# Mish in one ScalarE pass, logarithms of two head pairs at once, and three banks for the hidden product

## The chip, the cores and the metric

The kernel runs on one core of a Trainium2 chip. The metric is device time in microseconds (us), the median of several executions. TensorE multiplies matrices, VectorE and ScalarE work elementwise, SyncE only issues transfers (its queue is SPq in the rows), GpSimd is not used. PE stands for TensorE, PEld for its weight loads, DVE for VectorE, ACT for ScalarE.

## The reference, cut to what matters

```python
# q, k, v: [8, 8, 576, 64]; g_norm: [64]; w_in: [512, 2048]; w_out: [2048, 512]
kv  = einsum('bhsd,bhse->bhde', k, v)
a   = einsum('bhsd,bhde->bhse', q, kv)
a   = a / sqrt(mean(a * a, axis=-1, keepdims=True) + 1e-6) * g_norm
x   = a.transpose(0, 2, 1, 3).reshape(4608, 512)
h   = x @ w_in
out = (h * tanh(log1p(exp(h)))) @ w_out        # mish, then the second product
```

## The kernel before, in words

Everything is kept with features on the 128 partitions and tokens along the free dimension. The 4608 tokens are nine tiles of 512. x^T of a tile is made for four **head pairs** (128 features each) and then goes through 16 **chunks** of 128 hidden units. A float32 product runs as three passes of a faster format: each operand is split into a high part (a rounding copy on ScalarE, L85) and a low part (a subtraction on VectorE, L86).

**A chunk** is `hidden` (12 matmuls of 128x512 into one PSUM bank psh, L259 to L261, four quarters of the contraction with three passes each), `mish_a` and `mish_b` (elementwise, into gh and gl), and `project_out` (12 matmuls into the four banks acc, L288 to L290). The program traces them skewed: the hidden product of a chunk, mish_b of the chunk before it, then the second product of the chunk two steps back. `mish_a` is a chain that goes to and fro: Exp on ScalarE (L269), a clamp on VectorE (L270), Square on ScalarE (L271), (v + 0.5) h on VectorE (L272, the last reader of the bank psh), Ln and Exp on ScalarE (L273, L274); `mish_b` multiplies (L278) and splits. psh has two banks.

**x of the next tile** is made while a tile runs. `attention_slots` gives each step its slot, two slots per chunk: k^T v of a batch in two halves (L157, into a bank psa), and per head pair: load q, transpose, project (psa), square, sums over a head's features by a matmul with a matrix of ones (psa again), rstd (Ln at L242, Exp at L243), normalize (L246, then the split into xh and xl). psa has two banks; the projection's bank is held from its matmuls until L246.

**The first tile** has nothing to hide behind. The string START lists the order in which its loads, weight conversions and steps to x are traced; its projections go to the banks acc. A weight arrives as a float64 block (512 KB), and `weight` makes it float32: a scaling pass on ScalarE (L100), three integer passes on VectorE (L104 to L106, the last of which is the last reader of the raw block), then the split. The raw blocks (w64) have three buffers. Six blocks are in START, the other 26 are loaded in the chunks of the first tile, one of w_out per chunk and one of w_in until all 16 are there.

**The order on each engine** is not the program's: a scheduler goes through the traced instructions with a timeline of its own, and at each moment gives an engine the ready instruction that was traced first. On the chip each engine's queue then runs in that fixed order, and an instruction that waits holds up what is behind it. All loads and stores are issued by SyncE, in such an order too; a load waits there until its buffer is free.

The functions that the diff touches:

Of the kernel before, what the change touches and what calls it, by code (L numbers as in the profile page):

```python
# [7 lines left out]
F32 = mybir.dt.float32  # L8
F32R = mybir.dt.float32r
U32 = mybir.dt.uint32  # L10
AF = mybir.ActivationFunctionType
ALU = mybir.AluOpType
LB = -18 * 0.6931471805599453     # log(4 2^-20)


# the order in which the first tile starts. w, k, q: load weights, half of k and v,
# queries of a head pair; c: convert weights; m: k^T v; t, s, n: the steps to x
START = (
    "w0 k0 q0 q1 m0 t1 w1 t0 q2 s1 s0 c0 c1 w2 k1 m1 "
    "n1 t2 w3 n0 c2 w4 q3 s2 n2 c3 t3 s3 c4 w5 c5 n3"  # L20
# [4 lines left out]
def linear_attention_rms_mish_ffn(  # L25
# [20 lines left out]
    w_in, w_out = w_in.bitcast(U32), w_out.bitcast(U32)   # words of float64, low first  # L46
    P = 128
    T = 512                      # tokens of one tile of the feed-forward part
    NT = NTOK // T
    NKC = DM // P                # contraction chunks of x w_in, = head pairs  # L50
    NFC = DF // P                # chunks of the hidden dimension
    NSUB = T // P
    CM = 4                       # rows of k, v per partition in the main load
    SM = CM * P                  # rows in the main load
    SL = S - SM                  # rows left over

    T32 = 2                      # tiles whose x is made of unsplit operands
# [3 lines left out]
    wraw = ctx.enter_context(tc.tile_pool(name="wraw", bufs=3))  # L61
# [6 lines left out]
    ps_h = ctx.enter_context(tc.tile_pool(name="ps_h", bufs=2, space=bass.MemoryType.PSUM))  # L68
    ps_a = ctx.enter_context(tc.tile_pool(name="ps_a", bufs=2, space=bass.MemoryType.PSUM))
    ps_o = ctx.enter_context(tc.tile_pool(name="ps_o", bufs=1, space=bass.MemoryType.PSUM))  # L70

    nc.scalar.preload_act_table_set("natural_log_exp_and_others")
# [7 lines left out]
    eps = const.tile([P, 1], F32, name="eps")  # L80
    tiny = const.tile([P, 1], F32, name="tiny")
    lb = const.tile([P, 1], F32, name="lb")
# [6 lines left out]
    # The high word, read as a float32 and scaled by 2^-112, is the exponent  # L89
    # rebased to float32 and 20 bits of the mantissa, three places too low;  # L90
    # what float32 can't hold fades to zero.
# [41 lines left out]
    # Block-diagonal tiles of head pairs: the unsplit one of batch 0 or 1, and  # L133
    # the split ones, which batches two apart share.
# [56 lines left out]
    def unit_steps(j, hp, xh, xl):  # L191
# [31 lines left out]
        def square():  # L223
            t = ffn.tile([P, T], F32, name="n") if j == 0 else att.tile([P, T], F32, name="fa")
            nc.scalar.square(t, st["x"])
            if j < T32:
                st["sf"] = t
            else:
                st["sh"], st["sl"] = parts(t)

        def sums():
# [6 lines left out]
            st["ss"] = ps  # L238

        def rstd():  # L240
            st["r"] = att.tile([P, T], F32, name="fb")
            nc.scalar.activation(st["r"], st["ss"], AF.Ln, bias=eps, scale=1.0 / D)  # L242
            nc.scalar.activation(st["r"], st["r"], AF.Exp, scale=-0.5)  # L243

        def normalize():
            nc.vector.scalar_tensor_tensor(st["r"], st["x"], gcol, st["r"], ALU.mult, ALU.mult)  # L246
            split(xh[:, hp, :], xl[:, hp, :], st["r"])

        return load, transpose, project, square, sums, rstd, normalize
# [14 lines left out]
    # mish(h) = h tanh(log(1 + exp(h))) = 2 h t / (t^2 + 1), t = 1 + 2 exp(-h).  # L264
    # The bound on exp(-h) keeps log's argument in its range; tanh is 2^-41 there.
    def mish_a(ps):
        v = ffn.tile([P, T], F32, name="u")
        r = ffn.tile([P, T], F32, name="n")
        nc.scalar.activation(v, ps, AF.Exp, scale=-1.0)  # L269
        nc.vector.tensor_scalar_min(v, v, 2.0 ** 41)  # L270
        nc.scalar.activation(r, v, AF.Square, bias=1.0, scale=2.0)  # L271
        nc.vector.scalar_tensor_tensor(v, v, 0.5, ps, ALU.add, ALU.mult)  # L272
        nc.scalar.activation(r, r, AF.Ln, bias=tiny, scale=2.0 ** -20)  # L273
        nc.scalar.activation(r, r, AF.Exp, bias=lb, scale=-1.0)  # L274
# [161 lines left out]
```

## Time and profile before

| | |
|---|---|
| time, median of 3 runs | 923.93 us (922.19 to 928.57) |
| span of the profiled execution | 924.8 us (no time of its own is given beside it) |
| mean granted TensorE clock | 0.986 of full speed |
| TensorE busy | 896.3 us, 97% |
| ScalarE busy | 635.4 us, 69% |
| VectorE busy | 539.0 us, 58% |
| matmuls | 4348, of them 3456 of the two big products |
| chain that ended last | TensorE 94%, transfers 3% |

The span runs from the first to the last instruction. Matmuls are pipelined, so the busy time of one (about 0.39 us) is longer than the interval from start to start; the rate is read from how many begin in a stretch. An engine's busy share over the whole span says little here, since the first tile has other limits than the rest.

### The profile page before, as it was taken

The numbers are of one execution on the slowest core, as the hardware profiler recorded it, in microseconds if no ns is written. First come the engines' busy times: TensorE is split into PE (matmuls) and PEld (weight loads), VectorE is DVE, ScalarE is ACT, GpSimd is POOL, SyncE is SP. The second block draws the span as 40 slices with busy tenths as digits, with TensorE's granted clock in tenths as the row PEclk, the third lists the DMA queues.
The fourth block names the chain that finished last, engine by engine and source line by source line (L and its number), as shares of the span: only waits on it lengthen the run. The fifth ranks groups of instructions, "written<-read, shape, count | busy, mean of one in ns | idle before, by whom it ended". The sixth has DMA issues, their size and how long they took to land.

```text
span 924.8 us, 11829 instructions
## 1 busy us (share of the span) xinstructions
PE 896.3 (97%) x4348; PEld 717.2 (78%) x4348; DVE 539.0 (58%) x908; ACT 635.4 (69%) x1057; POOL 0.2 (0%) x4
## 2 busy tenths in 40 slices
PE   3789999999999999999999999999999999999997
PEld 1467778888888888888788878888888888888886
DVE  5889986565456544655466545554565456544443
ACT  3688877677667766776577666776676677766554
POOL 0000000000000000000000000000000000000000
PEclk9779999999999999999999999999999999999999
DMA  8964361200250005200430034002300030001001
GB/s 217 276 210 138 107 232 45 47 1 1 70 122 4 1 3 129 63 0 1 117 78 1 1 103 91 1 1 74 69 1 1 1 88 5 0 1 46 1 1 45
DMA packets 113434, 55.31 MB, mean 60 GB/s; under 512 B 88288, under 2 KB 104672, under 8 KB 113376
## 3 DMA queue, kind: packets, MB, share of 16 engines
q1 hardware_dynamic: 113376, 54.55, 21.4%
q8 instruction: 34, 0.56, 0.2%
q14 instruction: 24, 0.20, 0.1%
HBM read 45.09 MB, written 9.44 MB: 59 GB/s over the span
## 4 chain that ended last, share of the span: by engine, by line
PE 94%; DMA 3%; SPq 1%; DVE 1%; ACT 1%; issue 0%; ACTq 0%
PE psh L259 15%; PE acc L290 15%; PE acc L288 14%; PE acc L289 14%; PE psh L261 14%; PE psh L260 14%; PE psa L157 3%; DMA w<-in_moe_w_in_dram 2%; PE psa L220 1%; PE psa L219 1%; DMA vm<-in_v_dram 1%; PE psa L218 1%; SPq L185 1%; PE psa L237 1%; PE psa L236 1%; PE psa L215 1%
## 5 line engine op out<-in xcount | busy, mean ns | idle before, releaser
L259 PE MATMUL psh<-xh,wil 128*128 128x512 f32 x576 | 231.2, 402 | 2.2 <-ACT xh L85 2.2
L260 PE MATMUL psh<-xl,wih 128*128 128x512 f32 x576 | 228.2, 396 | 0.0
L261 PE MATMUL psh<-xh,wih 128*128 128x512 f32 x576 | 227.9, 396 | 0.0
L290 PE MATMUL acc<-woh,gh 128*128 128x512 f32 x576 | 227.6, 395 | 0.0
L289 PE MATMUL acc<-wol,gh 128*128 128x512 f32 x576 | 227.2, 394 | 0.0
L288 PE MATMUL acc<-woh,gl 128*128 128x512 f32 x576 | 223.4, 397 | 0.0
L86 DVE TENSOR_TENSOR gl<-n,gh 128x512 fp32r<-128x512 f32 x144 | 99.5, 691 | 84.7 <-ACT gh L85 81.5
L278 DVE TENSOR_TENSOR n<-u,n 128x512 f32<-128x512 f32 x144 | 99.3, 690 | 82.5 <-ACT n L274 82.3
L85 ACT CAST gh<-n 128x512 fp32r<-128x512 f32 x144 | 89.1, 618 | 82.2 <-DVE n L278 67.2
L272 DVE SCALAR_TENSOR_TENSOR u<-u,psh 128x512 f32<-128x512 f32 x144 | 98.8, 686 | 76.9 <-ACT n L271 76.8
L269 ACT ACTIVATE u<-psh 128x512 f32<-128x512 f32 x144 | 86.2, 598 | 78.6 <-PE psh L261 77.6
L259 PEld LDWEIGHTS psh<-xh,wil 128*128 128x128 f32 x576 | 108.9, 189 | 29.6 <-ACT xh L85 2.6
L260 PEld LDWEIGHTS psh<-xl,wih 128*128 128x128 f32 x576 | 109.1, 189 | 26.3 <-issue 0.9
L261 PEld LDWEIGHTS psh<-xh,wih 128*128 128x128 f32 x576 | 108.7, 189 | 25.8 <-issue 0.2
L289 PEld LDWEIGHTS acc<-wol,gh 128*128 128x128 f32 x576 | 108.5, 188 | 25.2 <-ACT u L269 0.4
L290 PEld LDWEIGHTS acc<-woh,gh 128*128 128x128 f32 x576 | 108.2, 188 | 25.4 <-issue 0.2
L288 PEld LDWEIGHTS acc<-woh,gl 128*128 128x128 f32 x576 | 108.2, 188 | 25.4 <-issue 0.4
L271 ACT ACTIVATE n<-u 128x512 f32<-128x512 f32 x144 | 90.8, 631 | 44.0 <-DVE u L270 42.9
L274 ACT ACTIVATE n<-n,lb 128x512 f32<-128x512 f32 x144 | 104.1, 723 | 3.6
L273 ACT ACTIVATE n<-n,tiny 128x512 f32<-128x512 f32 x144 | 104.1, 723 | 3.2
L270 DVE TENSOR_SCALAR u<-u 128x512 f32<-128x512 f32 x144 | 61.2, 425 | 68.9 <-ACT u L269 68.2
L86 DVE TENSOR_TENSOR fl<-fa,fh 128x512 fp32r<-128x512 f32 x56 | 38.6, 689 | 19.3 <-ACT fh L85 18.7
(61 smaller groups left out, 569.1 us busy)
## 6 DMA issues: line engine op xcount, KB each, us to landing
out_dram<-stg SPq DMA_DIRECT2D x36, 256.0 KB, 2.0
w<-in_moe_w_in_dram SPq DMA_DIRECT2D x16, 512.0 KB, 4.9
km<-in_k_dram SPq DMA_DIRECT2D x16, 512.0 KB, 4.0
vm<-in_v_dram SPq DMA_DIRECT2D x16, 512.0 KB, 5.4
w<-in_moe_w_out_dram SPq DMA_DIRECT2D x16, 512.0 KB, 3.9
stg<-in_q_dram SPq DMA_DIRECT2D x32, 64.0 KB, 2.4
stg<-in_q_dram SPq DMA_DIRECT2D x32, 56.0 KB, 2.0
stg<-in_q_dram SPq DMA_DIRECT2D x32, 48.0 KB, 1.9
```

The source lines that it names most:

```text
L86: nc.vector.tensor_sub(lo, src, hi.bitcast(F32))
L259: nc.tensor.matmul(ps, wil[:, kc, f], xh[:, kc, :], start=(kc == 0), stop=False)
L260: nc.tensor.matmul(ps, wih[:, kc, f], xl[:, kc, :], start=False, stop=False)
L261: nc.tensor.matmul(ps, wih[:, kc, f], xh[:, kc, :], start=False, stop=(kc == NKC - 1))
L271: nc.scalar.activation(r, v, AF.Square, bias=1.0, scale=2.0)
L272: nc.vector.scalar_tensor_tensor(v, v, 0.5, ps, ALU.add, ALU.mult)
L273: nc.scalar.activation(r, r, AF.Ln, bias=tiny, scale=2.0 ** -20)
L274: nc.scalar.activation(r, r, AF.Exp, bias=lb, scale=-1.0)
L278: nc.vector.tensor_mul(r, v, r)
L288: nc.tensor.matmul(acc[t], gl[:, c], woh[:, fc, :], start=first, stop=False)
L289: nc.tensor.matmul(acc[t], gh[:, c], wol[:, fc, :], start=False, stop=False)
L290: nc.tensor.matmul(acc[t], gh[:, c], woh[:, fc, :], start=False, stop=last)
```

## The change

- `mish_a` becomes one ScalarE pass with the function Mish, from psh to v; `mish_b` is left with the split.
- Mish is in another function table than Ln and Exp. `rstd` therefore takes two head pairs at once: an explicit load of the table with Ln and Exp, then Ln and Exp over 128x1024; the next Mish needs its own table again. A helper `in_turn` fixes the order of these ScalarE instructions among themselves to the traced one.
- To let a pair wait for its neighbour, x times g and the scaled sums are put into new SBUF tiles raw and ss (one buffer each for two pairs): after the square, VectorE writes raw = x g; after the sums, VectorE writes ss = sums / 64 + 1e-6; `normalize` is a plain product and the split. So a psa bank is free after those passes.
- Banks: psh 3 instead of 2, psa 1 instead of 2. Raw weight blocks: 2 buffers instead of 3.
- In START and in the slots, rstd stands by itself ("r"), and some steps move: c3 behind r3, c5 behind n3. The initial table load goes, and so do three constants.

```diff
-    "n1 t2 w3 n0 c2 w4 q3 s2 n2 c3 t3 s3 c4 w5 c5 n3"
+    "r1 t2 w3 n0 n1 c2 w4 q3 s2 t3 s3 r3 c3 n2 c4 w5 n3 c5"
...
-    wraw = ctx.enter_context(tc.tile_pool(name="wraw", bufs=3))
+    wraw = ctx.enter_context(tc.tile_pool(name="wraw", bufs=2))
...
-    ps_h = ctx.enter_context(tc.tile_pool(name="ps_h", bufs=2, space=bass.MemoryType.PSUM))
-    ps_a = ctx.enter_context(tc.tile_pool(name="ps_a", bufs=2, space=bass.MemoryType.PSUM))
+    xr = ctx.enter_context(tc.tile_pool(name="xr", bufs=1))
+    ps_h = ctx.enter_context(tc.tile_pool(name="ps_h", bufs=3, space=bass.MemoryType.PSUM))
+    ps_a = ctx.enter_context(tc.tile_pool(name="ps_a", bufs=1, space=bass.MemoryType.PSUM))
...
-    nc.scalar.preload_act_table_set("natural_log_exp_and_others")
...
+    def in_turn(i):
+        if last:
+            order = mybir.DependencyInfo(mybir.DependencyClass.NoSync, mybir.DependencyReason.DATA)
+            tc.add_manual_dep(i.ins, last.pop().ins.name, order, reason="tables")
+        last.append(i)
...
             nc.scalar.square(t, st["x"])
+            nc.vector.tensor_scalar_mul(raw[:, hp % 2, :], st["x"], gcol)
...
-            st["ss"] = ps
-
-        def rstd():
-            st["r"] = att.tile([P, T], F32, name="fb")
-            nc.scalar.activation(st["r"], st["ss"], AF.Ln, bias=eps, scale=1.0 / D)
-            nc.scalar.activation(st["r"], st["r"], AF.Exp, scale=-0.5)
+            nc.vector.tensor_scalar(ss[:, hp % 2, :], ps, 1.0 / D, 1e-6, ALU.mult, ALU.add)
 
         def normalize():
-            nc.vector.scalar_tensor_tensor(st["r"], st["x"], gcol, st["r"], ALU.mult, ALU.mult)
-            split(xh[:, hp, :], xl[:, hp, :], st["r"])
+            r = raw[:, hp % 2, :]
+            nc.vector.tensor_mul(r, r, ss[:, hp % 2, :])
+            split(xh[:, hp, :], xl[:, hp, :], r)
...
+    def rstd(ss):
+        in_turn(nc.scalar.preload_act_table_set("natural_log_exp_and_others"))
+        in_turn(nc.scalar.activation(ss, ss, AF.Ln))
+        in_turn(nc.scalar.activation(ss, ss, AF.Exp, scale=-0.5))
...
     def mish_a(ps):
         v = ffn.tile([P, T], F32, name="u")
-        r = ffn.tile([P, T], F32, name="n")
-        nc.scalar.activation(v, ps, AF.Exp, scale=-1.0)
-        nc.vector.tensor_scalar_min(v, v, 2.0 ** 41)
-        nc.scalar.activation(r, v, AF.Square, bias=1.0, scale=2.0)
-        nc.vector.scalar_tensor_tensor(v, v, 0.5, ps, ALU.add, ALU.mult)
-        nc.scalar.activation(r, r, AF.Ln, bias=tiny, scale=2.0 ** -20)
-        nc.scalar.activation(r, r, AF.Exp, bias=lb, scale=-1.0)
-        return v, r
+        in_turn(nc.scalar.activation(v, ps, AF.Mish))
+        return v
 
-    def mish_b(v, r):
-        nc.vector.tensor_mul(r, v, r)
+    def mish_b(v):
         gh = ffn.tile([P, T], F32R, name="gh")
         gl = ffn.tile([P, T], F32R, name="gl")
-        split(gh, gl, r)
+        split(gh, gl, v)
         return gh, gl
...
             s0 = 3 + 6 * hp
             slots[s0 - 1].append(start)
-            for d, n in zip((0, 2, 3, 4, 6, 11, 11), range(7)):
+            for d, n in zip((0, 2, 3, 4, 6), range(5)):
                 slots[s0 + d].append(lambda n=n, cell=cell: cell[n]())
+            e = 16 + 12 * (hp // 2)
+            if hp % 2 == 0:
+                slots[e + 1].append(lambda hp=hp: rstd(raws[j, hp // 2][1]))
+            slots[e + 3 + hp % 2].append(lambda cell=cell: cell[5]())
```

## Rows read from the trace of the kernel before

**Rows 1.** Stretches: busy us (instructions) per engine, clock, DMA; last row psh alone.

```profile
33.60:54.80 21.20, 15.65 (x112) 9.98 (x110) 19.21 (x35) 15.93 (x30) 0.00 (x0) 0.74 0.91 253
54.80:59.30 4.50, 4.50 (x15) 3.51 (x12) 4.38 (x10) 3.15 (x8) 0.00 (x0) 0.51 0.64 189
60.00:140.00 80.00, 80.00 (x400) 62.25 (x399) 75.02 (x139) 67.05 (x119) 0.00 (x0) 1.00 0.49 161
850.00:900.00 50.00, 50.00 (x217) 40.57 (x216) 22.42 (x36) 29.66 (x45) 0.00 (x0) 1.00 0.00 1
...
33.60:54.80 21.20, 8.61 (x24) 4.71 (x24) 1.37 (x2) 1.19 (x2) 0.74 0.91 253
```

**Rows 2.** Waits of TensorE, the longest of five: total us, times, longest.

```profile
PE psa L157 <- DMA vm<-in_v_dram: 17.1, 3, 10.8
```

**Rows 3.** Timeline of the opening: start us, us, engine, line, operation, operands.

```profile
33.60 1.83 PE L259 MATMUL psh<-xh,wil 128*128 128x512 f32 x2
...
44.10 0.69 DVE L86 TENSOR_TENSOR xl<-fb,xh 128x512 fp32r<-128x512 f32 x1 [0.34 <-ACT xh L85]
...
49.74 1.12 PE L157 MATMUL psa<-vm,km 128*64 128x64 f32 x16 [3.37 <-DMA vm<-in_v_dram]
49.75 0.69 DVE L272 SCALAR_TENSOR_TENSOR u<-u,psh 128x512 f32<-128x512 f32 x1
...
54.88 0.79 PE L259 MATMUL psh<-xh,wil 128*128 128x512 f32 x1
```

**Rows 4.** Chain that ended last, one half of a k^T v in steady state.

```profile
245.91 1.75 PE psa L157 x40
```

**Rows 5.** Groups by line, the mish: count | busy us, mean ns | idle before.

```profile
L273 ACT ACTIVATE n<-n,tiny 128x512 f32<-128x512 f32 x144 | 104.1, 723 | 3.2
...
L278 DVE TENSOR_TENSOR n<-u,n 128x512 f32<-128x512 f32 x144 | 99.3, 690 | 82.5 <-ACT n L274 82.3
L272 DVE SCALAR_TENSOR_TENSOR u<-u,psh 128x512 f32<-128x512 f32 x144 | 98.8, 686 | 76.9 <-ACT n L271 76.8
L271 ACT ACTIVATE n<-u 128x512 f32<-128x512 f32 x144 | 90.8, 631 | 44.0 <-DVE u L270 42.9 <-DVE gl L86 1.0
...
L269 ACT ACTIVATE u<-psh 128x512 f32<-128x512 f32 x144 | 86.2, 598 | 78.6 <-PE psh L261 77.6
```

**Rows 6.** Timeline of one late chunk, from its product to its use.

```profile
899.81 0.40 PE L261 MATMUL psh<-xh,wih 128*128 128x512 f32 x1
...
904.94 0.69 DVE L86 TENSOR_TENSOR gl<-n,gh 128x512 fp32r<-128x512 f32 x1 [0.74 <-ACT gh L85]
...
911.17 0.39 PE L288 MATMUL acc<-woh,gl 128*128 128x512 f32 x1
```

**Rows 7.** Timeline of the last chunk's low part and its first use.

```profile
916.08 0.69 DVE L86 TENSOR_TENSOR gl<-n,gh 128x512 fp32r<-128x512 f32 x1 [0.74 <-ACT gh L85]
...
916.82 0.50 PE L288 MATMUL acc<-woh,gl 128*128 128x512 f32 x1
```

**Rows 8.** Groups by line, the rms and the only table load.

```profile
L242 ACT ACTIVATE fb<-psa,eps 128x512 f32<-128x512 f32 x36 | 24.7, 686 | 1.1 <-PE psa L234 0.7 <-DVE xl L86 0.2
...
L246 DVE SCALAR_TENSOR_TENSOR fb<-psa,gcol,fb 128x512 f32<-128x512 f32 x32 | 23.9, 748 | 10.6 <-ACT fb L243 10.4
...
L72 ACT ACT_TABLE_LOAD x1 | 1.3, 1283 | 0.7 <-PEq L420 0.7
```

**Rows 9.** Waits of SyncE's queue: total us, times, longest.

```profile
SPq L94 <- DVE w L106: 51.4, 15, 6.0
```

**Rows 10.** Timeline of VectorE: last join pass of loads 7 and 25, split of 25.

```profile
36.52 0.68 DVE L106 SCALAR_TENSOR_TENSOR w<-w,w 128x512 uint32<-128x512 uint32 x1
...
118.88 0.68 DVE L106 SCALAR_TENSOR_TENSOR w<-w,w 128x512 uint32<-128x512 uint32 x1
...
122.17 0.68 DVE L86 TENSOR_TENSOR wil<-w,wih 128x512 fp32r<-128x512 f32 x1
```

**Rows 11.** Line L94, the 32 weight loads, from issue to landing.

```profile
DMA to landing us min/median/max: 3.1/4.4/6.9
```

More of the change, by code (lines that the diff above doesn't have):

```diff
@@ L12 @@
 ALU = mybir.AluOpType
-LB = -18 * 0.6931471805599453
 START = (
     "w0 k0 q0 q1 m0 t1 w1 t0 q2 s1 s0 c0 c1 w2 k1 m1 "
-    "n1 t2 w3 n0 c2 w4 q3 s2 n2 c3 t3 s3 c4 w5 c5 n3"
+    "r1 t2 w3 n0 n1 c2 w4 q3 s2 t3 s3 r3 c3 n2 c4 w5 n3 c5"
 )
@@ L79, in linear_attention_rms_mish_ffn @@
     ones = const.tile([P, P], F32R, name="ones")
-    eps = const.tile([P, 1], F32, name="eps")
-    tiny = const.tile([P, 1], F32, name="tiny")
-    lb = const.tile([P, 1], F32, name="lb")
     def split(hi, lo, src):
@@ L86, in split @@
         nc.vector.tensor_sub(lo, src, hi.bitcast(F32))
+    last = []
+    def in_turn(i):
[3 more added lines that the diff above has]
+        last.append(i)
     def weight(src, hi, lo):
@@ L189, in q_load, with unit_steps @@
         return t
-    def unit_steps(j, hp, xh, xl):
+    def unit_steps(j, hp, xh, xl, raw, ss):
         st = {}
@@ L223, in square @@
         def square():
-            t = ffn.tile([P, T], F32, name="n") if j == 0 else att.tile([P, T], F32, name="fa")
+            t = ffn.tile([P, T], F32, name="u") if j == 0 else att.tile([P, T], F32, name="fb")
             nc.scalar.square(t, st["x"])
+            nc.vector.tensor_scalar_mul(raw[:, hp % 2, :], st["x"], gcol)
             if j < T32:
@@ L237, in sums, with new_raw @@
                 nc.tensor.matmul(ps, ones, st["sh"], start=False, stop=True)
-            st["ss"] = ps
-        def rstd():
-            st["r"] = att.tile([P, T], F32, name="fb")
-            nc.scalar.activation(st["r"], st["ss"], AF.Ln, bias=eps, scale=1.0 / D)
-            nc.scalar.activation(st["r"], st["r"], AF.Exp, scale=-0.5)
-        def normalize():
-            nc.vector.scalar_tensor_tensor(st["r"], st["x"], gcol, st["r"], ALU.mult, ALU.mult)
-            split(xh[:, hp, :], xl[:, hp, :], st["r"])
-        return load, transpose, project, square, sums, rstd, normalize
+            nc.vector.tensor_scalar(ss[:, hp % 2, :], ps, 1.0 / D, 1e-6, ALU.mult, ALU.add)
+        def normalize():
+            r = raw[:, hp % 2, :]
+            nc.vector.tensor_mul(r, r, ss[:, hp % 2, :])
+            split(xh[:, hp, :], xl[:, hp, :], r)
+        return load, transpose, project, square, sums, normalize
+    def rstd(ss):
+        in_turn(nc.scalar.preload_act_table_set("natural_log_exp_and_others"))
+        in_turn(nc.scalar.activation(ss, ss, AF.Ln))
+        in_turn(nc.scalar.activation(ss, ss, AF.Exp, scale=-0.5))
+    def new_raw():
+        return (xr.tile([P, 2, T], F32, name="raw"), xr.tile([P, 2, T], F32, name="ss"))
     def new_x():
@@ L297, in linear_attention_rms_mish_ffn @@
     xs = {0: new_x()}
-    units = [unit_steps(0, hp, *xs[0]) for hp in range(NKC)]
+    raws = {(0, i): new_raw() for i in range(2)}
+    units = [unit_steps(0, hp, *xs[0], *raws[0, hp // 2]) for hp in range(NKC)]
     conv, kv_tiles = {}, {}
@@ L302, in linear_attention_rms_mish_ffn @@
         nc.sync.dma_start(gcol[r, :], g_norm.rearrange("(p o) -> p o", o=1))
-    nc.vector.memset(eps, 1e-6)
-    nc.vector.memset(tiny, 2.0 ** -20)
-    nc.vector.memset(lb, LB)
     nc.vector.memset(ones.bitcast(F32), 0.0)
@@ L310, in linear_attention_rms_mish_ffn @@
         n = int(n)
-        load, transpose, project, square, sums, rstd, normalize = units[n % NKC]
+        load, transpose, project, square, sums, normalize = units[n % NKC]
         if what == "w":
@@ L328, in linear_attention_rms_mish_ffn @@
             sums()
+        elif what == "r":
+            rstd(raws[0, n // 2][1])
         elif what == "n":
-            rstd()
             normalize()
@@ L357, in start @@
             def start(hp=hp, cell=cell):
-                cell.extend(unit_steps(j, hp, *xs[j]))
+                if hp % 2 == 0:
+                    raws[j, hp // 2] = new_raw()
+                cell.extend(unit_steps(j, hp, *xs[j], *raws[j, hp // 2]))
             s0 = 3 + 6 * hp
             slots[s0 - 1].append(start)
-            for d, n in zip((0, 2, 3, 4, 6, 11, 11), range(7)):
+            for d, n in zip((0, 2, 3, 4, 6), range(5)):
                 slots[s0 + d].append(lambda n=n, cell=cell: cell[n]())
+            e = 16 + 12 * (hp // 2)
+            if hp % 2 == 0:
+                slots[e + 1].append(lambda hp=hp: rstd(raws[j, hp // 2][1]))
+            slots[e + 3 + hp % 2].append(lambda cell=cell: cell[5]())
         return slots
@@ L384, in linear_attention_rms_mish_ffn @@
         if half is not None:
-            k0, *vr = half
-            ready.append((k0, mish_b(*vr)))
+            k0, vr = half
+            ready.append((k0, mish_b(vr)))
             half = None
         if step < NSTEP:
-            half = (step, *mish_a(ps))
+            half = (step, mish_a(ps))
             for w in conv:
```

## The prediction

> **What bounds the kernel now.** Read the stretches first [rows 1]. From 850 to 900 us TensorE starts 217 matmuls in 50 us at full clock, 0.2304 us each, while VectorE is busy for 22.4 us and ScalarE for 29.7 us; from 60 to 140 us it is just as full although VectorE is busy 75.0 of 80 us. So both engines that the change relieves have room in every tile but the first, and even there TensorE does not stand still. The waits of TensorE say the same from the other side: five in all, 23.6 us together, the longest by far for the loads of v [rows 2], and none after the start. Only the opening is left. Its rows [rows 3] show the first hidden matmul at 33.60, the last quarter of x (head pair 3) ready at 44.10 + 0.69 = 44.8, then a wait until 49.74 with the k^T v of batch 1 at the head of TensorE's queue, and dense hidden matmuls from 54.88 on only.
>
> How much is to be had there? In the 21.28 us from 33.60 to 54.88 TensorE did 24 hidden matmuls [rows 1], worth 24 x 0.2304 = 5.5 us at full rate, two halves of a k^T v of 40 matmuls at 1.75 us [rows 4], and the other eight of its 112, float32 matmuls of projections and sums, between 1.8 and 3.7 us (once and twice a hidden one; 2.2 taken, since two are narrow). That is 11.2 us; 10.1 us are idle time or half clock. From 54.8 to 59.3 us the granted clock is 0.51 [rows 1], the lower of the two levels, after the idle stretch: 4.5 x (1 - 0.51), some 2 us more. The whole opening can give back about 12 us with x ready as now, and nothing later can give anything.
>
> **The mish.** Removed per chunk [rows 5]: a Square and two ScalarE passes (0.631 + 2 x 0.723 = 2.08 us; Ln and the last Exp have equal rows, one is shown) and on VectorE the clamp, L272 and L278 (the last two 1.38 us). The Exp pass from PSUM becomes a Mish pass. Its function is not in the trace; the passes of other functions run from 0.598 to 0.723 us, and I take 0.60, since L269 has its very source, size and destination. Over 144 chunks that is some 300 us of ScalarE and at least 198 us of VectorE. In the steady tiles its worth is read from one chunk [rows 6]: the last hidden matmul starts at 899.81, the low part is ready at 904.94 + 0.69 = 905.63, and the second product reads it at 911.17. So 5.5 us of slack already hide the old chain; shortening it to 0.60 + 0.62 + 0.69 plus hand-overs, about 2.3 us, only lengthens the slack to about 9 us. Worth in 143 chunks: nothing. At the end of the program the low part lands within 0.1 us of its matmul [rows 7]; 0.2 us, left out of the sum.
>
> At the start it matters. The third chunk could not begin before L272 had read the first bank, from 49.75 to 50.44 [rows 3]. With Mish the bank is free one pass after its last matmul, and there are three banks: TensorE can run three quarters of three chunks, 27 matmuls, before x's last quarter comes, and go on after it.
>
> **The opening summed up.** Ceiling: x complete at 44.8 as now, 27 hidden matmuls done, then dense. Of the 10.08 us to 54.88, 1.75 go to the second k^T v half and 1.0 to a projection; 7.33 / 0.2304 gives 31 matmuls, 58 instead of 24, worth 34 x 0.2304 = 7.8 us, and 2.0 for the clock: 9.8 us. Floor of the same case: v lands at 49.74 again and stands ahead of the third or fourth chunk; the nine matmuls after 44.8 end at 46.9, 2.9 us are lost, and the clock may drop as now: 9.8 - 2.9 - 2.0 = 4.9 us. I take 5.5, near the floor, because DMA is at 0.91 of its share in this stretch [rows 1]: shuffling loads will not make v much earlier.
>
> **The rms.** Per head pair VectorE gets three passes (x times g, the scaling of the sums, the product) and loses one. Each is like L278 at 0.690, the lost one is 0.748 [rows 5, 8]: +1.3 us, 5.3 us for tile 0, where VectorE is busy 19.2 of 21.2 us. On the path of the last quarter lie the scaling and the product instead of the fused product, +0.63; the rest is somewhere between 0 and 4.7. Against it, Ln of pair 3 no longer waits until pair 2 has left fb, which by the code has one buffer. I take both as equal, with -3 to +3 us kept for the range. In the steady tiles it is 5.3 us a tile on a VectorE that the mish alone keeps busy for 22.4 of 50 us [rows 1], and of that over half goes: nothing.
>
> **Table loads.** 18 visits to Ln and Exp, each with a load before and one after. A load took 1.283 us, seen once [rows 8]. Ln and Exp over twice the columns are between once and twice 0.686, so a visit occupies ScalarE for at most 2 x 1.283 + 2 x 1.37 = 5.3 us. Queued behind it are the next Mish, the rounding copies of gh and the squares; TensorE waits for these only after 9 us of slack. Cost nothing; if that cover were gone, up to 5.3 us a visit. The Trainium skill, page "ScalarE: Activation LUTs", section "What ACT_TABLE_LOAD costs", gives about 2.66 us for a switch, a drain of 1.38 us included, and its section "Table sets: the hidden batching unit" says to group work by set, which the old chain did and the new one does not. By that figure a visit would be 8.1 us, still under 9 us. No row here shows a switch in mid-kernel.
>
> **One bank for projections and sums.** A projection's bank is now free after the square and the product with g, and sums after one VectorE pass, where a bank used to wait for Ln, Exp and the final product. The next user is a few chunks away. Between no loss and one 0.69 us pass exposed per use (ten uses a tile, eight tiles: 55 us); I take 0, because TensorE had no wait at all after the start and the readers are emptier now.
>
> **Two weight buffers for three.** SyncE's loads wait for the last join pass of an earlier weight: 15 times, 51.4 us [rows 9]. Between the joins of the 7th and the 25th load, 37.20 to 119.56 [rows 10], 18 loads went at 4.58 us each. Two buffers keep this rhythm if one cycle takes under 9.15 us: landing 4.4 us (3.1 to 6.9) [rows 11], a scaling pass on ScalarE (0.60 to 0.72 by [rows 5]) and three join passes of at most 0.68 us [rows 10], 7.1 us without queueing. That leaves 2 us, and a VectorE freed of mish. Cost nothing, narrowly. k, v and q queued behind these loads on SyncE wait with them.
>
> **Sum.** The profile gives a span of 924.8, and no separate time around it; it lies 0.9 above the median of 923.93, inside the spread of the runs. 924.8 - 5.5 = 919.3; on the median 918.4, and I say 918.5. One per cent, 9.2 us, is about what a measurement of this kernel can tell from no change.
>
> **Rivals.**
> - *Nothing gained in the opening* (922 to 925): loads of k, v and q set when x is complete, and the added VectorE passes eat the rest. For it: DMA share 0.91 and VectorE 19.2 of 21.2 us. Against it: a chunk's bank held until 50.44, which does go away. Chance 0.22.
> - *The whole ceiling and an earlier x* (909 to 914): with fewer weights ahead of it, batch 0's k and v land earlier, x is complete 2 to 5 us sooner, and TensorE runs dense: 924.8 - 9.8 - 2 to 5. Against it the same DMA share. Chance 0.22.
> - *Weights become the bound, slower*: above 9.15 us a cycle the 25th load falls behind its use. Its low part is ready at 122.17 + 0.68 [rows 10], 3.3 us after its last join, and TensorE is full there, so there is little to spare. Four hand-overs each behind one 0.69 us pass would make 10.0 us; 18 x 0.43 = 7.7 us lost, and at 10.7 us a cycle 14: 932 to 938. It decides at 9.15. Chance 0.09.
> - *Switching tables stalls TensorE, slower*: if ScalarE reaches a visit late, because the sums come late, 1 to 2 us of a visit's 5.3 stick out, 18 times: 937 to 955. The batching rule of "ScalarE: Activation LUTs" in the Trainium skill would make this likely; the slack in [rows 6] speaks against. Chance 0.05.
>
> The forecast itself (915 to 922) has 0.42.
>
> **How the numbers follow.** Faster by over 1% (under 914.7) is the second rival and the low end of the forecast: 0.25. Slower by over 1% (over 933.2): most of the last two, 0.11. Range: from the middle of the ceiling case, 909, to the start of the weights case, 931.
>
> **What would show it.** Right: after 60 us no wait of TensorE, 0.23 us a matmul; ScalarE some 250 us and VectorE some 200 us less busy, with the time hardly moved; dense hidden matmuls from about 45 to 50 us. Wrong: waits on psa, on a Mish or on wil in TensorE's rows after 60 us; x complete later than 47 us; a cycle of weights above 9.15 us.

## The result and the profile after

The changed kernel takes 931.54 us (930.00 to 933.04, five runs); the kernel before, in five runs on the same chip, 925.91 us (922.19 to 928.57). The ratio is 1.0075 with an interval of 1.0047 to 1.0104: 0.75% slower, where 0.6% faster was forecast. The profiled execution took 931.2 us, its span is 929.4 us, 4.6 us more than before, at the same mean clock of 0.986. ScalarE is busy for 393 us instead of 635, VectorE for 337 instead of 539.

Stretches of the changed kernel, as in [rows 1]; the last row counts the hidden matmuls alone:

```profile
33.60:54.80 21.20, 13.49 (x70) 8.88 (x69) 17.09 (x31) 10.11 (x19) 0.00 (x0) 0.74 0.84 228
54.80:59.30 4.50, 4.50 (x40) 3.42 (x39) 3.03 (x6) 3.61 (x6) 0.00 (x0) 0.82 0.69 193
60.00:140.00 80.00, 80.00 (x338) 62.51 (x337) 66.02 (x116) 48.93 (x85) 0.00 (x0) 1.00 0.48 150
850.00:900.00 50.00, 50.00 (x216) 40.23 (x215) 6.24 (x9) 10.97 (x18) 0.00 (x0) 1.00 0.00 0
...
33.60:54.80 21.20, 8.60 (x24) 5.76 (x23) 0.00 (x0) 0.74 0.84 228
```

The opening is no better: 24 hidden matmuls again from 33.60 to 54.80, and the transfers fill 0.84 of their share where 0.91 was seen. After 60 us TensorE is always busy, as before. And yet one matmul fewer starts between 850 and 900 us, while VectorE and ScalarE are nearly idle.

Waits of TensorE, against [rows 2]; the single row behind them is one of the waits for v in the kernel before, from its timeline:

```profile
PE psa L160 <- DMA vm<-in_v_dram: 11.5, 1, 11.5
PE psa L160 <- DVE ss L242: 3.5, 2, 2.7
PE psh L268 <- ACT xh L79: 3.2, 1, 3.2
PE psa L238 <- DVE ss L242: 3.2, 1, 3.2
PE psa L238 <- ACT u L228: 1.7, 1, 1.7
```

```profile
24.24 0.69 PE L157 MATMUL psa<-vm,km 128*64 128x64 f32 x16 [2.97 <-DMA vm<-in_v_dram]
```

The longest wait for v is the start of the program in both kernels: 10.8 us in [rows 2], 11.5 us here. The two waits for v inside the opening, 2.97 us at 24.24 and 3.37 us at 49.74 in [rows 3], are gone. In their place stand three waits for `ss`, the pass that frees the only bank psa (3.2 us and 3.5 us in two rows), and one for `xh`. All lie before 52 us. Timeline of the opening, against [rows 3]:

```profile
23.24 2.05 PE L238 MATMUL psa<-u,ones 128*128 128x512 f32 x2 [3.22 <-DVE ss L242]
...
28.62 1.28 ACT L253 ACT_TABLE_LOAD   x1
29.92 0.53 ACT L164 COPY kvh<-psa 64x128 f32<-64x128 f32 x2
...
30.50 2.08 PE L218 MATMUL acc<-u,kvh 128*128 128x512 f32 x2 [1.44 <-ACT kvh L164]
...
34.66 0.70 DVE L208 STREAM_TRANSPOSE u<-stg 128x512 f32<-128x512 f32 x1
...
39.02 0.67 ACT L103 ACTIVATE w<-w 128x512 f32<-128x512 f32 x1 [4.23 <-DMA w<-in_moe_w_in_dram]
39.05 1.02 PE L218 MATMUL acc<-u,kvh 128*128 128x512 f32 x2
...
40.61 0.67 ACT L103 ACTIVATE w<-w 128x512 f32<-128x512 f32 x1 [0.92 <-DMA w<-in_moe_w_in_dram]
...
41.18 0.57 ACT L228 ACTIVATE u<-acc 128x512 f32<-128x512 f32 x1
...
44.95 0.68 DVE L242 TENSOR_SCALAR ss<-psa 128x512 f32<-128x512 f32 x1
...
46.10 0.67 ACT L103 ACTIVATE w<-w 128x512 f32<-128x512 f32 x1 [1.03 <-DMA w<-in_moe_w_out_dram]
...
46.67 1.05 ACT L254 ACTIVATE ss<-ss 128x1024 f32<-128x1024 f32 x1
47.75 1.06 ACT L255 ACTIVATE ss<-ss 128x1024 f32<-128x1024 f32 x1
...
51.51 1.65 PE L268 MATMUL psh<-xh,wil 128*128 128x512 f32 x3 [3.22 <-ACT xh L79]
...
52.18 1.28 DVE L80 TENSOR_TENSOR xl<-raw,xh 128x512 fp32r<-128x512 f32 x2
```

Read it from the end. x is complete at 52.18 + 1.28 = 53.46, against 44.8 before. Ln of the last two pairs (46.67) waits for the last sums (44.95) and for a scaling pass ahead of it on ScalarE (46.10). The sums wait for a square (41.18), that for the last projection (39.05), which stands in TensorE's queue behind 18 hidden matmuls, and its transposition (34.66) in VectorE's queue behind other work. In the kernel before these three ran at 29.02 (transposition), 30.97 (projection) and 32.92 (square): the 8 us are lost there. Ahead of that the second sums waited 3.22 us for the bank, and at 28.62 ScalarE loads a table that it has already (Ln and Exp of the first two pairs have just run), before the copies for which TensorE waits 1.44 us. Then ScalarE stands for 4.23 us at a weight that lands late, and for 0.92 us at the next one, with the last square behind both. Little of that lies on the path to x: the projection ends at 39.05 + 1.02 = 40.07, so the square (41.18) loses 1.1 us, and Ln about 1 us behind the scaling pass at 46.10.

Steady state: groups by line, against [rows 5, 8]. The rows are Mish, the scaling of the sums, the load of the table with Ln and Exp, and Ln.

```profile
L275 ACT ACTIVATE u<-psh 128x512 f32<-128x512 f32 x144 | 86.1, 598 | 212.8 <-PE psh L270 211.1 <-DVE gl L80 1.3
L242 DVE TENSOR_SCALAR ss<-psa 128x512 f32<-128x512 f32 x36 | 24.8, 690 | 113.2 <-PE psa L241 112.1 <-PE psa L238 1.0
...
L253 ACT ACT_TABLE_LOAD x18 | 23.1, 1283 | 1.0 <-PEq L425 0.7
...
L254 ACT ACTIVATE ss<-ss 128x1024 f32<-128x1024 f32 x18 | 19.1, 1059 | 1.3 <-DVE ss L242 1.1
```

Timeline, first of a visit to the other table, then of one late chunk, against [rows 6]; the first and the last row are the start of the second product in the third tile and the last matmul of all:

```profile
258.40 0.40 PE L288 MATMUL acc<-woh,gl 128*128 128x512 f32 x1
...
333.02 1.28 ACT L253 ACT_TABLE_LOAD   x1
334.32 1.06 ACT L254 ACTIVATE ss<-ss 128x1024 f32<-128x1024 f32 x1
...
904.32 0.39 PE L270 MATMUL psh<-xh,wih 128*128 128x512 f32 x1
...
904.75 0.60 ACT L275 ACTIVATE u<-psh 128x512 f32<-128x512 f32 x1 [2.12 <-PE psh L270]
...
908.26 0.69 DVE L80 TENSOR_TENSOR gl<-u,gh 128x512 fp32r<-128x512 f32 x1 [4.91 <-ACT gh L79]
...
915.75 0.40 PE L288 MATMUL acc<-woh,gl 128*128 128x512 f32 x1
...
923.92 0.40 PE L290 MATMUL acc<-woh,gh 128*128 128x512 f32 x1
```

The same two points of the kernel before:

```profile
256.07 0.40 PE L288 MATMUL acc<-woh,gl 128*128 128x512 f32 x1
...
919.48 0.40 PE L290 MATMUL acc<-woh,gh 128*128 128x512 f32 x1
```

They split the loss. The third tile's second product begins 258.40 - 256.07 = 2.3 us later; from there to the last matmul it takes 665.52 us instead of 663.41, 2.1 us more, without a wait. The second part is the strange one: the same matmuls in both, some 2650 of them of the two big products, but a start-to-start interval in tiles 3 to 7 of 235.1 ns (second product) and 233.6 ns (hidden) instead of 234.2 and 232.8 (means over 960 each, worked out from the start times).

The weights, against [rows 9, 10, 11]. Waits of SyncE's queue, and the landing of line L97:

```profile
SPq L97 <- DVE w L109: 64.3, 22, 6.8
```

```profile
DMA to landing us min/median/max: 3.1/3.8/6.3
```

Last join pass of loads 7 and 25 (timeline of VectorE):

```profile
43.74 0.68 DVE L109 SCALAR_TENSOR_TENSOR w<-w,w 128x512 uint32<-128x512 uint32 x1
...
115.64 0.68 DVE L109 SCALAR_TENSOR_TENSOR w<-w,w 128x512 uint32<-128x512 uint32 x1
```

18 loads in 71.90 us make 3.99 us each, 8.0 us a cycle of two buffers; but the seventh is done 7.2 us later than in [rows 10].

### The profile page after: what moved, and what is told of

Same layout as the page of the kernel before. It is cut to its first block, busy times and chain, and to the rows that moved or that the text cites. A ratio compares the mean times of both kernels' runs of the same rounds, so it can differ in the third digit from the quotient of the medians.

```text
span 929.4 us, 11093 instructions
## 1 busy us (share of the span) xinstructions
PE 898.6 (97%) x4348; PEld 716.6 (77%) x4348; DVE 336.8 (36%) x545; ACT 392.7 (42%) x623; POOL 0.2 (0%) x4
## 4 chain that ended last, share of the span: by engine, by line
PE 94%; SPq 1%; DMA 1%; ACT 1%; DVE 1%; issue 1%; ACTq 0%; DVEq 0%
PE psh L268 15%; PE acc L289 14%; PE acc L288 14%; PE acc L290 14%; PE psh L269 14%; PE psh L270 14%; PE psa L160 2%; SPq L188 1%; DMA w<-in_moe_w_in_dram 1%; PE psa L223 1%; PE psa L222 1%; PE psa L221 1%; PE psa L241 1%; PE psa L240 1%; PE psa L238 1%
## 5 line engine op out<-in xcount | busy, mean ns | idle before, releaser
L80 DVE TENSOR_TENSOR gl<-u,gh 128x512 fp32r<-128x512 f32 x144 | 98.8, 686 | 281.0 <-ACT gh L79 279.8
L79 ACT CAST gh<-u 128x512 fp32r<-128x512 f32 x144 | 88.8, 618 | 171.5 <-PE acc L290 171.3
L242 DVE TENSOR_SCALAR ss<-psa 128x512 f32<-128x512 f32 x36 | 24.8, 690 | 113.2 <-PE psa L241 112.1
L229 DVE TENSOR_SCALAR raw<-psa,gcol 128x512 f32<-128x512 f32 x32 | 23.9, 746 | 50.1 <-ACT fb L228 49.1
L208 DVE STREAM_TRANSPOSE fa<-stg 128x512 f32<-128x512 f32 x32 | 22.7, 711 | 47.2 <-DMA stg<-in_q_dram 43.9
L160 PE MATMUL psa<-vm,km 128*64 128x64 f32 x512 | 24.5, 243 | 15.1 <-DMA vm<-in_v_dram 11.5
L160 PEld LDWEIGHTS psa<-vm,km 128*64 128x64 f32 x512 | 19.7, 150 | 23.8 <-issue 13.7
L103 ACT ACTIVATE w<-w 128x512 f32<-128x512 f32 x32 | 21.5, 672 | 37.0 <-DMA w<-in_moe_w_in_dram 25.5
L80 DVE TENSOR_TENSOR xl<-raw,xh 128x512 fp32r<-128x512 f32 x36 | 24.6, 690 | 25.4 <-ACT xh L79 24.2
```

The source lines that it names most:

```text
L79: nc.scalar.copy(hi, src)
L80: nc.vector.tensor_sub(lo, src, hi.bitcast(F32))
L160: nc.tensor.matmul(ps[o * D:(o + 1) * D, i, :], kt, vt, start=(c == 0), stop=(c == CM))
L229: nc.vector.tensor_scalar_mul(raw[:, hp % 2, :], st["x"], gcol)
L242: nc.vector.tensor_scalar(ss[:, hp % 2, :], ps, 1.0 / D, 1e-6, ALU.mult, ALU.add)
```

## The experiments

Three things could hold what was lost. **Places**: the three constants that went took 32 bytes a partition each in the buffer layout; behind them everything that transfers fill, x and the chunk buffers (u, gh, gl) lies 96 bytes lower, besides whole multiples of 4096 bytes (x 4192 bytes lower by the tile sizes in the code: one raw weight buffer of 4096 bytes, and 96). **Weights**: two raw buffers. **x**: one bank, the order of the steps, the extra load. The rivals were that Mish itself, or its table visits, cost it.

All results in one table. "x" is the end of the fourth low part of x; "60 us" the matmuls of the two big products started by then; "tile 3" the start of its second product; "rest" from there to the start of the last matmul (all worked out from start times in each trace; one profiled execution each). The ratio is to the kernel before on the same chip; its medians there run from 925.2 to 925.9, so medians of kernels from different chips compare to within some 0.7 us.

| kernel | median us | ratio (95%) | x | 60 us | tile 3 | rest |
|---|---|---|---|---|---|---|
| before | 925.91 | | 44.79 | 38 | 256.07 | 663.41 |
| changed | 931.54 | 1.0075 (1.0047 to 1.0104) | 53.47 | 37 | 258.40 | 665.52 |
| 1 changed, 96 bytes back | 926.69 | 1.0010 (0.9998 to 1.0021) | 52.43 | 40 | 257.09 | 662.93 |
| 2 before, 32 bytes on | 934.52 | 1.0096 (1.0080 to 1.0112) | 48.79 | 30 | 259.39 | 666.71 |
| 3 before, 64 bytes on | 928.69 | 1.0029 (1.0013 to 1.0045) | 46.90 | 29 | 259.53 | 663.70 |
| 4 before, x 32 on, chunk 64 on | 921.78 | 0.9955 (0.9940 to 0.9971) | 44.31 | 52 | 252.19 | 661.64 |
| 5 before, chunk 64 on | 922.74 | 0.9974 (0.9962 to 0.9985) | 46.14 | 41 | 254.54 | 661.19 |
| 6 changed, chunk 96 on | 928.93 | 1.0047 (1.0033 to 1.0060) | 54.72 | 36 | 258.30 | 663.67 |
| 7 before with Mish | 925.90 | 1.0009 (0.9997 to 1.0021) | 45.98 | 61 | 252.32 | 666.66 |
| 8 before, two weight buffers | 935.15 | 1.0108 (1.0091 to 1.0124) | 42.31 | 67 | 264.18 | 663.41 |
| 9 kernel 7, two weight buffers | 934.41 | 1.0101 (1.0082 to 1.0121) | 44.24 | 68 | 261.16 | 666.66 |
| 10 kernel 1, raw moved | 926.95 | 1.0022 (1.0013 to 1.0032) | 51.28 | 47 | 255.96 | 662.93 |
| 11 kernel 1, three weight buffers | 929.86 | 1.0042 (1.0028 to 1.0056) | 54.21 | 36 | 258.90 | 662.93 |
| 12 kernel 1, sums in psh | 929.47 | 1.0051 (1.0037 to 1.0065) | 48.85 | 47 | 257.09 | 662.93 |
| 13 kernel 12, no second load, chunk 64 on | 929.57 | 1.0060 (1.0042 to 1.0078) | 44.01 | 58 | 260.70 | 660.51 |
| 14 kernel 11, sums in psh, no second load | 923.90 | 0.9989 (0.9972 to 1.0006) | 51.75 | 53 | 253.81 | 662.93 |
| 15 kernel 14, chunk 64 on | 921.71 | 0.9967 (0.9953 to 0.9980) | 50.80 | 50 | 253.33 | 660.51 |

The last column is telling by itself. Kernels 1, 10, 11, 12 and 14 differ in their openings, banks and weights; their x and chunk buffers lie in the same places, or all 4096 bytes higher: 662.93 in all five. With the chunk buffers 64 bytes on it is 660.51 in both. As this part repeats so exactly, the scatter between executions (922.19 to 928.57 in the kernel before) has to lie mostly ahead of the third tile: a difference of a microsecond or two in the columns "x", "60 us" and "tile 3" is not to be read by itself.

### The places of the buffers (kernels 1 to 6)

Kernel 1 puts three unused constants back; the order of the instructions on TensorE, ScalarE, VectorE and SyncE stays that of the changed kernel.

```diff
+    pads = [const.tile([P, 1], F32, name=f"pad{i}") for i in range(3)]
```

> The changed kernel with three unused 32-byte constants put back, so that every buffer behind the constants starts 96 bytes later, at a multiple of 64 bytes again; the instruction order of TensorE, VectorE and ScalarE is the same. Address theory (the three removed constants moved x and gh off a 64-byte boundary and each matmul takes 1.2 ns longer): steady interval between matmuls back from 233.3 to 232.0 ns, the steady tile back from about 98.2 to 97.8 us, span 3 to 4 us shorter, near 926. Traffic theory (the interval comes from what ScalarE and VectorE now do): interval stays at 233.3 ns, span at 929.

Measured: 4.85 us faster than the changed kernel. Its two points:

```profile
257.09 0.40 PE L289 MATMUL acc<-woh,gl 128*128 128x512 f32 x1
...
920.02 0.39 PE L291 MATMUL acc<-woh,gh 128*128 128x512 f32 x1
```

In these two executions 1.3 us come back before the third tile and 2.6 us after it. Of the loss, this is nearly all: the time is 1.0010 of before, with 1 inside the interval. It is what the theory of places expected; the rival that what ScalarE and VectorE now do slows the matmuls is out, since they do the same here.

Kernel 2 adds one unused constant of 32 bytes to the kernel before, and nothing else.

```diff
+    pad = const.tile([P, 1], F32, name="pad")
```

> The kernel before with one more 32-byte constant, so that everything behind it starts 32 bytes off a 64-byte boundary, as in the changed kernel; same instruction order. Address theory: interval 233.3 instead of 232.0 ns, time 3 to 5 us longer (ratio 1.004). Traffic theory: no change, ratio 1.000.

Measured: 1% slower. Its two points:

```profile
259.39 0.40 PE L289 MATMUL acc<-woh,gl 128*128 128x512 f32 x1
...
926.10 0.40 PE L291 MATMUL acc<-woh,gh 128*128 128x512 f32 x1
```

3.3 us are lost in the first two tiles and 3.3 us after; x is complete 4.0 us later. The transfers themselves are slower: the 14336 packets of 128 bytes that start in the first 60 us (the loads of q) take 14.72 ns each instead of 12.88 (means worked out from the packets in each trace), while the passes are not: the join passes take 684 ns instead of 685. What the buffers hold, who uses them and the order on every engine are the same; the place alone costs it.

Which buffers? Kernel 3 shifts by 64 bytes (`pad` of 16 floats), kernel 4 leaves the buffers of the transfers and shifts x by 32 and the chunk buffers by 64 bytes, kernel 5 the chunk buffers alone by 64, and kernel 6 takes the changed kernel and shifts the chunk buffers alone by 96 (a pad in a pool of its own between the pools). The cut shows kernel 5.

```diff
     xp = ctx.enter_context(tc.tile_pool(name="xp", bufs=2))
+    pb = ctx.enter_context(tc.tile_pool(name="pb", bufs=1))
...
+    padg = pb.tile([P, 16], F32, name="padg")
```

> The kernel before with everything behind the constants 64 bytes later instead of 32; same instruction order. If what counts is a boundary of 64 bytes: ratio 1.000, interval 232.0 ns. If it is one of 128 bytes or more: ratio 1.005 to 1.010, interval near 233.3 ns.

> The kernel before with only xh and xl 32 bytes later (a 32-byte buffer ahead of them, another behind them, so that what follows lies 64 bytes later): the buffers that transfers write stay on their boundary. If the matmuls read x in 64-byte pieces and transfers are the other half of the loss: interval of the hidden product up by about 1.2 ns, that of the second product not, 1728 x 1.2 = 2.1 us, opening unchanged, ratio 1.002. If the matmul interval depends on gh and gl: 232.0 ns, ratio 1.000. If x alone sets it for both products: ratio 1.005.

> The kernel before with 64 bytes between the buffers of x and those of the chunk (u, n, gh, gl and what follows), x and all that transfers fill staying in place. Theory that each product has its own offset (x sets the interval of the hidden product, gh and gl that of the second): 12 matmuls of the second product 2750 to 2765 ns instead of 2783, of the hidden one 2784 as before; 144 x 18 to 33 ns, 2.6 to 4.8 us less, ratio 0.995 to 0.997. Theory that only the distance between x and the rest counts: both move.

> The changed kernel with 96 bytes in front of the buffers of the chunk alone: gh and gl are back where their 64-byte remainder was, x and the buffers that transfers fill stay 32 bytes off. Own-offset theory: 12 matmuls of the second product 2783 ns again (2803 in the changed kernel), the hidden product stays near 2797; 144 x 20 ns = 2.9 of the 4.9 us that the full pad gave, time near 928.6. If transfers to buffers off a boundary carry most of it: within 1 us of the changed kernel's 931.5.

Measured: with the transfer buffers in place nothing is lost in the opening (252.19 and 254.54); with these 64 bytes on it is lost (259.53), while the rest stays within 0.3 us. The packets say the same without exception: in the thirteen kernels of the table whose transfer buffers lie as before (or a whole 4096 bytes off) those of 128 bytes take 12.84 to 13.00 ns; in the four where they are moved, 13.85 (changed), 14.72 (kernel 2), 15.71 (kernel 3) and 15.33 (kernel 6).

The chunk buffers 64 bytes on make the rest 2.2 us shorter than before; put back alone in the changed kernel they return 665.52 - 663.67 = 1.85 of the 2.6 us. Kernels 4 and 5 differ in the place of x alone: 32 bytes cost 661.64 - 661.19 = 0.45 us. So the interval of the matmuls goes with the places of x and of the chunk buffers, the opening with those of the transfers. There is no simple order (64 is worse than 0 for all together, better for the chunk buffers alone), and kernel 5 speaks against the theory that each product has its own offset: with only the chunk buffers and what lies behind them moved, the second product goes from 234.2 to 232.3 ns, but the hidden product, which reads none of these, from 232.8 to 233.4 ns. Kernel 3 (1.0029) fits neither of its two expectations, and kernel 4 is faster than any of its three. Which accesses meet is not settled.

### Mish alone (kernel 7)

The kernel before with Mish in place of the chain, a table load only where the function changes, its banks and buffers as they were.

```diff
+        in_turn(nc.scalar.activation(v, ps, AF.Mish))
+        table[0] = "mish"
+        return v
```

> The kernel before with the Mish function alone: rms per head pair as before (four switches of tables a tile there and back), banks 2 + 2, three weight buffers, all constants kept in place. Theory that Mish itself helps the opening: 3 to 6 us faster. Theory that it only empties engines that had room: within 2 us. Theory that switches of tables stall TensorE: slower by 5 us or more, with waits of TensorE after 150 us.

Measured: no change in all, in two halves. In the opening it does what the forecast hoped for: 61 big matmuls by 60 us instead of 38, and the third tile 3.75 us sooner. After that it loses 3.25 us, without a wait of TensorE. In tiles 3 to 7 the 360 short matmuls of k^T v take 17.4 instead of 15.8 us in all and the hidden ones 234.5 instead of 232.8 ns each; hidden matmuls now run in the middle of a k^T v half, eight times, where [rows 4] shows 40 in one piece. The places are those of before, and kernel 1 runs Mish in the old places without this loss (662.93 us, 15.8 us for the same 360). That leaves the order of the instructions, or the 66 table loads where kernel 1 has 35; that it is the splitting that slows them was not tried by itself.

### Two weight buffers (kernels 8 and 9)

The third raw buffer gives way to an unused tile of its size, so that all else stays in place.

```diff
-    wraw = ctx.enter_context(tc.tile_pool(name="wraw", bufs=3))
+    wraw = ctx.enter_context(tc.tile_pool(name="wraw", bufs=2))
...
+    hole = const.tile([P, 1024], F32, name="hole")
```

> The kernel before with two raw weight buffers instead of three, the freed 4096 bytes held so that no address moves. Theory that two weight buffers delay x of the first tile (ScalarE and VectorE stand in their queues before weights that land late): x complete some 3 to 6 us later and time 2 to 6 us longer. Theory that the one psa bank and the rms passes do it: within 1.5 us.

> The kernel before with Mish alone and two raw weight buffers instead of three, addresses kept. In the kernel before, two buffers cost 9.6 us. Theory that this cost came with a VectorE full of mish and goes with it: at most 2 us over the Mish kernel's 925.9. Theory that two buffers are too few once the opening is early: 4 to 10 us over it, with waits of TensorE for wil, woh or Mish between 60 and 150 us.

Measured: 9.6 and 8.5 us slower, more than either expectation for kernel 8, and x does not come later in it, as was expected, but earlier. Stretch and waits of TensorE in kernel 8:

```profile
60.00:160.00 100.00, 87.87 (x420) 66.38 (x419) 89.03 (x160) 77.13 (x133) 0.00 (x0) 0.98 0.42 137
```

```profile
PE psh L260 <- DVE wil L87: 5.0, 2, 2.8
PE acc L289 <- ACT woh L86: 4.1, 4, 1.8
...
PE psh L260 <- DVE u L273: 2.0, 2, 1.1
...
PE acc L290 <- DVE wol L87: 0.8, 1, 0.8
```

It is a good opening and a bad first tile: 67 big matmuls by 60 us, x at 42.31, and then 12.1 us of 100 in which TensorE stands: 9.9 us in waits for weights (wil, woh, wol), 2.0 us for the old chain's last reader of the bank (L273 here). From the 7th to the 25th load a cycle takes 9.48 us (42.91 to 128.19, by nine), over the 9.15 at which the prediction let it decide. But kernel 9 loses nearly as much with 8.21 us a cycle (44.83 to 118.69), so that threshold does not hold. In both the rest of the program is the same to 0.01 us as with three buffers.

### The rest of the changed kernel's opening (kernels 10 to 15)

Kernel 10 makes room: `raw` moves into fh and fl (tiles 1 and 2) and later into a raw weight buffer that is no longer used. Kernel 11 spends the room on the third weight buffer. Kernel 12 is kernel 1 with the first tile's sums in the banks psh. Kernel 13 adds to kernel 12 the last hunk, no load of a table that is there; kernel 14 adds both these edits to kernel 11. Kernels 13 and 15 also have the pad of 64 bytes.

```diff
+            r = [att.tile([P, T], F32, name=n) for n in ("fh", "fl")]
...
-            ps = ps_a.tile([P, T], F32, name="psa")
+            ps = ps_h.tile([P, T], F32, name="psh") if j == 0 else ps_a.tile([P, T], F32, name="psa")
...
-        in_turn(nc.scalar.preload_act_table_set("natural_log_exp_and_others"))
+        if table[0] != "ln":
+            in_turn(nc.scalar.preload_act_table_set("natural_log_exp_and_others"))
+            table[0] = "ln"
```

> The padded changed kernel, two weight buffers, with x times g in fh and fl for tiles 0 and 1 and in a weight buffer later, as in the run with three buffers. Theory that this move cost the 3.2 us by which that run lay above the padded kernel: 929 to 932, and the third buffer gave 0 to 2 us. Theory that the move is free: 926.7 as the padded kernel, and the third buffer itself put the first tile into a slower order.

> The padded changed kernel with three raw weight buffers again; the 4096 bytes come from x times g, which lies in fh and fl for tiles 0 and 1 and in a weight buffer from tile 2 on (all weights are in by then). Theory that two weight buffers eat what the opening gains: x of the first tile complete 3 to 8 us sooner than with two, time 918 to 922 (ratio 0.992 to 0.996). Theory that the single psa bank and the rms passes delay x: within 2 us of the padded kernel, ratio 1.000.

> The padded changed kernel with one edit: the sums of the first tile go to psh banks, idle then, instead of the one psa bank. Single-bank theory (the sums and the k^T v of the first tile queue for one bank, TensorE waits 6.7 us for ss): no such wait, x of the first tile 3 us or more sooner, 3 to 6 us less, 921 to 924. Theory that the loads set x anyway: within 1.5 us of the padded kernel's 926.7.

> The padded changed kernel with the sums of the first tile in psh banks, without the second load of a table that is there already, and with 64 bytes more in front of the chunk's buffers. If all three add: 926.7 - 4 (bank and load) - 2.6 to 4.8 (second product at 2750 to 2765 ns per 12) = 918 to 920, ratio 0.992 to 0.994. If the opening does not answer: 922 to 924.

> The same with two more edits for the first tile: its four sums go to the psh banks, which are idle then, instead of the one psa bank, and the second visit to Ln and Exp does not load the table that is there already (a load of 1.28 us stood on the chain). Single-bank theory: another 2 to 5 us less, near 916, no wait of TensorE for ss in the opening. Weight-buffer theory alone: within 1.5 us of the run before it.

> The run with three weight buffers, sums of the first tile in psh banks and no second table load (923.9 us), with 64 bytes more ahead of the chunk's buffers. If the address effect adds: 12 matmuls of the second product 2750 to 2765 ns instead of 2783, 919 to 921 us, ratio 0.994 to 0.995. If not (the hidden product slows by as much, as in the padded kernel with this offset): 923 to 925.

Measured: the move is free (926.95). Kernels 11, 12 and 13 were expected to be faster than kernel 1, and all three are slower: the third buffer alone costs 2.9 us, the sums in psh alone 2.8 us, though x is complete 3.6 us earlier. In kernel 11 the single bank holds TensorE for longer, 5.6 + 2.6 us of waits for `ss` where kernel 1 has 3.3 + 3.4. The 2.8 us of kernel 12 are not in its trace, as its profiled execution (927.38) was its fastest and spans what kernel 1's does; kernel 13, which has the same edit, shows what comes next:

```profile
60.00:160.00 100.00, 94.02 (x414) 69.81 (x413) 76.10 (x132) 57.81 (x95) 0.00 (x0) 1.00 0.40 130
```

```profile
PE psh L275 <- ACT u L282: 5.4, 5, 2.1
...
PE acc L296 <- ACT woh L82: 1.6, 3, 0.6
```

x is complete at 44.0 us and 58 big matmuls have begun by 60 us, and in the next 100 us TensorE stands for 6.0 us, for weights and for Mish passes that wait on ScalarE between them. With three buffers the same edits pay (kernel 14, 2.8 us less than kernel 1; kernel 15 against 13 is 7.9 us). So in the changed kernel x and the weights bind in turn, and either cure alone gains nothing. Kernel 14 was expected near 916 and came to 923.90. Kernel 15 is the fastest form of the change found, 0.3% under the kernel before, and no faster than the kernel before with its buffers moved (kernel 4).

## Why the prediction was wrong

The forecast was 918.5, the result 931.54, 13.0 us more. Of that, 925.91 - 923.93 = 2.0 us lie in the base, which came out higher over five runs. 931.54 - 926.69 = 4.85 us are places. The other 6.2 us are the opening: -5.4 us from the base was forecast, and kernel 1, which has the old places, is 0.8 us above it (1.0010 of the kernel before on its own chip). So two steps failed: the buffers' places, put at nothing without a reason, and x of the first tile, taken as ready at 44.8 us.

One reading in the sum was wrong too, and cost nothing, as the sum takes a difference: a span is not to be set against a median time as it stands. The changed kernel's span of 929.4 us is 1.8 us shorter than the time of the same execution (931.2), so the span of 924.8 belongs to an execution of some 926.6 us. And the 10.8 us wait for v lies at the start of the program, ahead of the opening; the waits of [rows 2] are seven, in five rows.

**What bounds the kernel.** "Nothing later can give anything" held as far as waits go: there are none after 60 us. But it took the 0.2304 us a matmul for a constant, and it is not one. That "three constants go" was listed in the change and had no term in the sum. Nothing in the old trace shows what it costs; but where the matmul interval is the time, the question which edits move buffers could have been asked. Shown by kernels 1 and 2.

**The mish.** Right. The pass takes 598 ns, as the Exp from the same bank did. The slack of a chunk did not grow to 9 us but from 5.5 to 915.75 - 908.95 = 6.8 us, since the copy to gh now waits for its buffer; either way it is worth nothing in a steady tile. That Mish and a freed bank help in the opening is right as well, shown by kernel 7 (23 more big matmuls by 60 us where 34 was the ceiling).

**The opening summed up; the rms.** The sum rests on x complete at 44.8, "with -3 to +3 us". It was 53.46 (52.43 with the old places), and this step failed first; "x complete later than 47 us" was a sign of being wrong that the prediction itself named. The added passes were not the trouble (x is at 44.0 in kernel 13, which has them all). What was missed is the order: the last projection came 8 us later in the queues, and the sums in psh bring it forward (29.06 us in kernel 12). Ln for two pairs at once also waits for the later pair: here 46.67, after sums at 44.95.

**One bank.** "I take 0, because TensorE had no wait at all after the start." The reason holds after the start, but the bank matters in the opening: 3.2 + 3.5 us of waits for `ss`. With the sums in psh x is complete 3.6 us earlier (kernel 12 against 1).

**Table loads.** Right in the steady tiles: 18 and 17 loads of 1.283 us and no wait of TensorE. From the start of a load to the start of Ln it is 334.32 - 333.02 = 1.30 us. The page "ScalarE: Activation LUTs" of the Trainium skill, section "What ACT_TABLE_LOAD costs", counts a drain of 1.38 us besides; this row shows none, and the row decides. Not priced was a load of the table already there, in the opening, ahead of copies that TensorE waits for. Kernels 13, 14 and 15 leave it out together with other edits, so its worth alone stays open.

**Two weight buffers.** "Cost nothing, narrowly" is wrong as a statement on the buffers: they cost 8 to 10 us wherever x is early (kernels 8 and 9; 13 against 15). The rival with 0.09 had the mechanism, TensorE waiting for weights. That its 932 to 938 held the 935.15 of kernel 8 was luck: a cycle of 9.48 us is 0.33 over its threshold, nine times that is 3.0 us, and kernels 9 and 13 lose 8.5 and 7.9 us with cycles of 8.21 and 8.07, under it. What the threshold left out, as far as the traces show, is the start: with two buffers the 7th load is done at 42.91 (kernel 8), 44.83 (kernel 9) and 49.2 us (kernel 13) instead of 37.20. In the changed kernel the cost is hidden, as x is late anyway, and the third buffer alone gives nothing (kernel 11). But two buffers also hold back the sixth load, issued at 32.60 where before it was 24.1, and that is the weight for which ScalarE stood 4.23 us ahead of the last square; of these, about 1.1 us reached the square.

**The rivals.** "Nothing gained in the opening" (0.22) is what happened in kernel 1, though its reason (transfers at 0.91, VectorE full) is not: in the changed kernel both have more room than before (0.84, and 17.1 of 21.2 us). The time fell outside the range by 0.5 us because the places came on top.

## What to carry to other kernels

Where an engine runs without waits for hundreds of microseconds, its interval is the time, and an edit that only moves buffers can change it by half a per cent, here once by one: compare against a version padded to the old places before giving a difference to the algorithm. When two resources bind in turn in a short opening (here x and the weight buffers), a fix of either alone reads as zero or worse, so try them together before writing one off. A resource taken away in exchange for another (a bank, a buffer) has to be priced in the stage that uses it hardest, not in the steady state.

## What the hardware showed that was not expected

The interval of back-to-back 128x512 matmuls depends on where the buffers lie: 662.93 us for the same rest of the program with one set of places, 665.52 with x and the chunk buffers 96 bytes lower, 660.51 with the chunk buffers 64 bytes higher, and 666.71 for the kernel before with all 32 bytes higher (663.41 in place). It is not only a matter of a matmul's own operands: the chunk buffers 64 bytes higher also change the hidden product, which does not read them (232.8 to 233.4 ns). Transfers into moved buffers are slower, too: packets of 128 bytes take 12.84 to 13.00 ns in the thirteen kernels with these buffers in place, 13.85 to 15.71 ns in the four with them moved by 32, 64 or 96 bytes. The third tile then begins 3.3 or 3.5 us later (kernels 2 and 3). Which rule stands behind either was not found.
